# Retention and a Mish layer on one core: chunks 10 to 13 transposed by transfers, three loads moved behind them, two sums moved ahead of two scalings

## The chip, the cores and the metric

The kernel runs on one core of one Trainium2 chip. The metric is the device time of one execution in microseconds; the kernel before takes 295.73 us (median of 3 runs, 295.64 to 296.11). One more execution was taken with the hardware profiler, and all durations below come from it.

The core's engines have a queue each and run side by side: PE (TensorE, matrix products into the PSUM banks), DVE (VectorE), ACT (ScalarE), POOL (GpSimd) and SP (SyncE). Each takes its instructions strictly in the order written. POOL and SP also issue DMAs: an instruction that waits at the head of such a queue holds every DMA behind it.

## The reference

Inputs are q, k and v of shape (8, 8, 576, 64), that is batch, heads, positions, head size, and two weights of 512 x 2048 and 2048 x 512, all float32.

```python
scores = (1 / sqrt(64)) * q @ k.transpose(0, 1, 3, 2)
gamma  = 1 - 2 ** (-5 - arange(8))                 # one decay a head
Dmat   = where(i >= j, gamma ** (i - j), 0)        # causal decay
x      = (scores * Dmat) @ v                       # no softmax
x      = x.transpose(0, 2, 1, 3).reshape(4608, 512)
h      = x @ w_in
out    = (h * tanh(softplus(h))) @ w_out           # Mish between two products
```

## The kernel before

**Chunks and tiles.** Each of the 8 sequences of 576 positions is cut into four chunks of 128 and one of 64; the 64s of two sequences share a chunk. That gives 36 chunks, numbered in the order of work, and four of them make a tile of 512 tokens (nine tiles, `t`). Chunks 0 to 7 are the first chunks of all sequences and have a special path. From chunk 8 on (`N0 = 8`; the source writes chunk 10 as `N0 + 2`) the retention is done by states: a running sum of k times v for each sequence, of which every half chunk (64 positions) needs the state before it. Chunk 14 is one of the shared ones, so its loads come in half transfers (six instead of three); 12, 13, 15 and 16 are plain.

**Steps of one chunk `n`.** They are plain functions, and whoever calls them decides the order on each engine's queue, since nothing reorders the instructions.

- `load(n)` issues the DMAs of q, k and v from POOL's queue into `qkraw` and `vraw`, and remembers the last one, that of v, in `landed[n]`.
- `step_p(n)` scales q and k by their decays on DVE into `qks` (bf16; two instructions, L324).
- `step_v(n)` scales v on DVE (L331).
- `step_t(n)` turns `qks` into `qkT`, head size along the partitions. For `n < NT` (11) PE does this with eight transposes (L345) into a PSUM bank, and ACT copies them out in two parts (L346, L347). From `NT` on it is a transposing DMA from SBUF to SBUF, issued from SP (L349), which may be told to wait for another instruction (`gate`).
- `step_s(n)` makes the scores of chunks `n` and `n + 1` on PE (L363), first those of `n`, then those of `n + 1`; it needs both `qkT`.
- `step_m(n)` masks them on DVE (L369).
- `states(n)` multiplies k by v for the new states on PE (L418). It leaves a job, `sum_up`, in the list `sums`: four or so additions on DVE (L442, L452, L454) into `total`. That one leaves a cast of the totals to bf16 in the list `casts` (L457, `ssb`). `run(sums)` and `run(casts, engine)` place them in the queues.
- `outputs(n)` and `outputs_end(n)` multiply the masked scores and the states into the outputs on PE (L477, L494).
- `hold(n)` is a copy of one column of `qkT` on POOL (L512, `held`). It does nothing useful but wait for the transposing DMA of `n`, and with it POOL's queue waits.

**A visit.** `visit(n)` stands for a pair of chunks, `n` and `n + 1`, and mixes the outputs of this pair with the scores and states of the next pair on PE, in this order: first unit of `states(n + 2)`; `outputs(n)`; the first half of `outputs_end(n)`; `step_s(n + 2)`; further units; the second half of `outputs_end(n)`; the rest. The second half has to wait for all products of the first half (two halves share a bank). That wait is carried by a no-op on SP: `written` puts it there (L394), it waits for PE's products, and PE's second half waits for it. So the no-op stands in SP's queue between the transposing DMAs and the stores.

**The stretch that is changed.** After the first tile, a loop runs `u` from 0 to 23. For `u < 16` it does `g1(1, u)`, the first product and Mish (ACT, L580) of the second tile; then `g2(1, u - 16)`, a quarter of a row block of its second product. Around these the tables `ps`, `vs` and `ts_` say at which `u` which chunk gets `step_p`, `step_v` and `step_t`; the visit to 8 is at `u == 17`, that to 10 at `u == 22`. Loads of 12 and 13 are issued at `u` 4 and 8, 14 at 9, 15 at 18 and 16 at 20; a `hold(13)` stands at `u == 17`. Then the main loop runs over tiles `t` from 2 and steps `i`: the visit to 12 is at `t = 2, i = 6`, and `step_p` and `step_t` of 16 at `i = 1`. Loads of 17 and 18 wait for the Mish of products (2, 2) and (2, 3) (`gated`).

**Split products.** `halved[0]` is a count of products that `product` does in two halves of 256 columns instead of one of 512 (L548 instead of L543). The result is the same, with two instructions more (a matmul and a weight load).

Of the kernel before, what the change touches and what calls it, by code (L numbers as in the profile page):

```python
# [10 lines left out]
BF16 = mybir.dt.bfloat16  # L11
# [5 lines left out]
def kernel(  # L17
# [21 lines left out]
    P = 128  # L39
    NP = H // 2  # L40
# [3 lines left out]
    KC = d_model // P  # L44
    NCH = 4
    NPE = 18
    NT = 11
    NV = 20
    PF = 5

# [10 lines left out]
    N0 = 2 * NCH  # L61
# [11 lines left out]
    ps_sc = ctx.enter_context(tc.tile_pool(name="ps_sc", bufs=2, space=PS))  # L73
    ps_st = ctx.enter_context(tc.tile_pool(name="ps_st", bufs=1, space=PS))
# [215 lines left out]
    landed = {}  # L290

    def load(n, gate=None):
        if n >= n_chunks:
            return
        b, c = chunks[n]
        qkr = io.tile([P, 2, H, D], F32, name="qkraw")
        vr = io.tile([P, H, D], F32, name="vraw", bufs=6)
        live[n] = {"qkr": qkr, "v": vr}
        for t, src in ((qkr[:, 0], q), (qkr[:, 1], k), (vr, v)):
            if c < 4:  # L300
                ins = nc.gpsimd.dma_start(  # L301
                    out=t, in_=src[b, :, ds(P * c, P), :].rearrange("h p d -> p h d"))
                if gate is not None:
                    behind(ins, gate)
                    gate = None
            else:
                for e in range(2):
                    ins = nc.gpsimd.dma_start(
                        out=t[ds(64 * e, 64)],
                        in_=src[b + e, :, ds(512, 64), :].rearrange("h p d -> p h d"))  # L310
                    if gate is not None:
                        behind(ins, gate)
                        gate = None
        landed[n] = ins
# [21 lines left out]
    def step_t(n, gate=None):  # L336
        flat = live[n]["qks"].rearrange("p i h d -> p (i h d)")
        qk = tr.tile([P, 2, NP, P], BF16, name="qkT", bufs=6)
        if n < NT:
            if n == N0 + 2:  # L340
                tp = ps_st.tile([P, 2 * NP, P], BF16, name="st")
            else:
                tp = ps_sc.tile([P, 4 * NP, P], BF16, name="sc")[:, 0:2 * NP]
            for i in range(2 * NP):
                nc.tensor.transpose(tp[:, i, :], flat[:, ts(i, P)], ident)  # L345
            nc.scalar.copy(qk[:, 0], tp[:, 0:NP])  # L346
            later.append(lambda: nc.scalar.copy(qk[:, 1], tp[:, NP:2 * NP]))  # L347
        else:
            ins = nc.sync.dma_start_transpose(out=qk.rearrange("p i n t -> p (i n) t"), in_=flat)  # L349
            if gate is not None:  # L350
                behind(ins, gate)
        live[n]["qk"] = qk

    def step_s(n):

        sc = ps_sc.tile([P, 2, 2, NP, 64], F32, name="sc")
        for x in range(2):
            qk = live[n + x]["qk"]
            for p in range(NP):
                for e in range(2):  # L360
                    for j in range(2):
                        r, i = ds(64 * e, 64), ds(64 * j, 64)
                        nc.tensor.matmul(sc[i, e, x, p, :], lhsT=qk[r, 1, p, i], rhs=qk[r, 0, p, i],  # L363
                                         start=True, stop=True, skip_group_check=True)
        live[n]["sc"] = sc

    def step_m(n):
        sm = tr.tile([P, 2, 2, NP, 64], BF16, name="sm", bufs=2)
        nc.vector.tensor_tensor(  # L369
            sm.rearrange("p e x n i -> p (e x n) i"), live[n]["sc"].rearrange("p e x n i -> p (e x n) i"),  # L370
            mask.unsqueeze(1).to_broadcast([P, 4 * NP, 64]), op=OP.mult)
        live[n]["sm"] = sm
# [3 lines left out]
    def flush():  # L376
        while later:
            later.pop()()
# [5 lines left out]
    sums = []  # L384
    casts = []

    def behind(ins, others):

        sync = mybir.DependencyInfo(mybir.DependencyClass.Sync, mybir.DependencyReason.DATA)
        tc.add_manual_dep(ins.ins, others.ins.name, sync, reason="row halves and a bank")  # L390

    def written(products):
        sync = mybir.DependencyInfo(mybir.DependencyClass.Sync, mybir.DependencyReason.DATA)
        seen = nc.sync.nop()  # L394
        for ins in products:
            tc.add_manual_dep(seen.ins, ins.ins.name, sync, reason="row halves and a bank")
        return seen
# [64 lines left out]
    def run(jobs, *how):  # L462
        while jobs:
            jobs.pop()(*how)
# [45 lines left out]
    def hold(n):  # L510

        nc.gpsimd.tensor_copy(held[:, n % 2:n % 2 + 1], live[n]["qk"][:, 1, NP - 1, P - 1:P])  # L512

    def visit(n, banks, copies, between=None):


        units, early = states(n + 2)
        if units:
            units[0]()
        both = outputs(n, banks)  # L520
        seen = written(outputs_end(n, both, 0))
        if units:
            step_s(n + 2)
        elif between:
            between()
        for unit in units[1:early]:
            unit()
        outputs_end(n, both, 1, seen)
        for unit in units[max(early, 1):]:
            unit()  # L530
        outputs_copy(n, both, copies)
        if units:
            step_m(n + 2)

    outs = {}
    halved = [0]
# [65 lines left out]
    def stores(copy=nc.vector.tensor_copy):  # L602
        while ready:
            store(*ready.pop(), copy)
# [25 lines left out]
    def store(t, s, ops, copy):  # L630
        ot = op.tile([P, d_model], F32, name="res")
        copy(ot, ops)  # L632
        b, c = chunks[NCH * t + s]
        if c < 4:
            nc.sync.dma_start(out=out[ds(b * S + P * c, P), :], in_=ot)
        else:
            for e in range(2):
                nc.sync.dma_start(out=out[ds((b + e) * S + 512, 64), :], in_=ot[ds(64 * e, 64), :])

    def att(n, steps):  # L640
        if n >= n_chunks:
            return
        for step in steps:
            {"P": step_p, "V": step_v, "T": step_t}[step](n)
# [69 lines left out]
    for i in range(nF):  # L714
        for step in steps.get(i, "").split():
            n = int(step[1])
# [14 lines left out]
    queued = [4 * NCH]  # L731
# [5 lines left out]
                queued[0] += 1  # L737


    ps = {0: (0,), 4: (1,), 8: (2,), 11: (5,), 14: (6,), 23: (7,)}  # L740
    vs = {0: (0,), 5: (1,), 18: (4,), 19: (5,)}
    ts_ = {3: (0,), 7: (1,), 10: (3, 4), 12: (2,), 17: (5,), 18: (6,)}
    for u in range(24):
        j, w = divmod(u, 4)
        halved[0] = 2 if 0 < u < 9 or 11 < u < 16 else 4 if 15 < u < 18 else 0
        if u == 9:
            att(N0 + 2, "V")
            att(N0 + 3, "PV")
            att(N0 + 4, "P")
            load(N0 + 6)  # L750
        for n in ps.get(u, ()):
            att(N0 + n, "P")
        if u == 11:
            step_m(N0)
        for n in vs.get(u, ()):
            att(N0 + n, "V")
        if u == 18:
            load(N0 + 7)
        if w == 0 and j in (1, 2, 5):
            if j < 5:  # L760
                load(N0 + j + 3)
            else:
                load(N0 + j + 3)
                queued[0] += 1
        if u == 10:
            units, early = states(N0)
            seen = written(units[0]())
            step_s(N0)
            units[1]()
            units[2](seen)  # L770
            run(sums)
        elif u == 17:
            visit(N0, ((ps_o, "ops"), (ps_h, "hp")), (act, act))
            run(sums)
        elif u == 22:
            visit(N0 + 2, ((ps_h, "hp"), (ps_h, "hp")), (act, dve))
        elif u == 23:
            att(N0 + 7, "T")
        if u == 20:
            stores(act)  # L780
        if u in (13, 20):
            run(casts, dve if u == 13 else act)
        for n in ts_.get(u, ()):
            step_t(N0 + n, landed[N0 + 6] if n == 3 else None)
        if u == 17:
            hold(N0 + 5)
        stores()
        if u < nF:
            g1(1, u, 2 if u == 0 else 1)
            flush()  # L790
        else:
            g2(1, u - nF)
# [3 lines left out]
    for t in range(2, nT + 1):  # L796
        for i in range(nF):
            n, w = NCH * (t + 1) + i // 8 * 2, i % 8
# [19 lines left out]
            if w == 7 and n + 4 <= NPE + 2:  # L818
                step_t(n + 5, newest[0])
# [74 lines left out]
```

## Time and profile before

| | |
|---|---|
| median of 3 runs | 295.73 us (295.64 to 296.11) |
| the profiled execution, its own time | 296.05 us |
| its span, first to last instruction | 294.3 us |
| PE busy | 288.2 us (98%) |
| DVE, ACT, POOL busy | 140.7, 125.0, 125.0 us (48%, 42%, 42%) |
| granted TensorE clock | 1.0 |
| DMA, mean over the span | 164 GB/s, 48.23 MB |
| loop over `u` in the trace | about 47 to 73.5 us |
| visits to 8, 10 and 12 on PE | from 64.5, 70.5 and 82.5 us |

Lines of the profile read like this: start or busy time in microseconds, the engine, the line of the source, the operation, the tiles as out<-in, and the count; in brackets the idle time of the engine ahead of the instruction and what ended it. `SPq` is SP's queue; the duration of a DMA there or on POOL is that of its issue, not of the transfer. "DMA to landing" is the time from the issue to the last byte's arrival.

### The profile page before, as it was taken

How to read it: one execution, taken by the hardware profiler on the slowest of the kernel's cores; microseconds unless marked ns; L12 is line 12 of the kernel's file. 1: busy time of each engine (PE TensorE's matmuls, PEld its weight loads, DVE VectorE, ACT ScalarE, POOL GpSimd, SP SyncE). 2: the span in 40 equal slices, each digit the busy share in tenths (PEclk: the TensorE clock that was granted, in tenths of full speed). 3: DMA queues.
4: the chain of work that ended last, by engine and by line, in shares of the span. 5: the costliest groups of instructions: out<-in, count | busy, mean ns of one | idle time of the engine just before them, and what ended most of it. 6: DMA issues, size and time to landing. Idle time of an engine off the chain costs nothing.

```text
span 294.3 us, 7942 instructions
## 1 busy us (share of the span) xinstructions
PE 288.2 (98%) x3485; PEld 160.5 (55%) x3485; DVE 140.7 (48%) x252; ACT 125.0 (42%) x206; POOL 125.0 (42%) x164
## 2 busy tenths in 40 slices
PE   8999999999899999999999999999999999999995
PEld 5666887665557454547545454545454544444443
DVE  6851659787763838454645454535453321000011
ACT  4866126764545534443444434343435333333200
POOL 8944769705267294955484536392020000000000
PEclk9999999999999999999999999999999999999999
DMA  7999999958798999899576838374222111011121
GB/s 157 236 202 205 205 327 357 328 136 178 220 249 236 148 243 225 248 158 309 131 209 176 247 90 256 94 222 120 70 64 71 38 38 65 9 36 44 62 74 71
DMA packets 47235, 48.23 MB, mean 164 GB/s; under 512 B 29152, under 2 KB 36320, under 8 KB 47200
## 3 DMA queue, kind: packets, MB, share of 16 engines
q0 software_dynamic: 15120, 31.20, 41.7%
q1 hardware_dynamic: 31936, 16.32, 22.6%
q8 instruction: 27, 0.44, 0.7%
q10 hardware_dynamic: 144, 0.20, 0.2%
q14 instruction: 8, 0.07, 0.1%
HBM read 37.75 MB, written 9.44 MB: 160 GB/s over the span
## 4 chain that ended last, share of the span: by engine, by line
PE 90%; DVE 4%; DMA 3%; ACT 1%; POOL 1%; issue 0%; POOLq 0%; DVEq 0%
PE hp L543 38%; PE ops L543 30%; PE hp L548 7%; PE ops L548 3%; DMA qkraw<-in_k_dram 2%; PE sc L363 1%; PE hp L624 1%; PE hp L494 1%; PE st L548 1%; PE sc L418 1%; PE hp L477 1%; DMA qkT<-qks 1%; DVE total L454 1%; PE st L418 1%; PE sc L200 1%; PE sc L222 1%
## 5 line engine op out<-in xcount | busy, mean ns | idle before, releaser
L543 PE MATMUL hp<-xT,w_in_t 128*128 128x512 bf16 (+1 forms) x508 | 126.0, 376 | 0.9 <-ACT gT L580 0.9
L580 ACT ACTIVATE gT<-hp 128x512 bf16<-128x512 f32 x142 | 84.6, 597 | 95.1 <-PE hp L543 94.2
L543 PE MATMUL ops<-w_out_t,gT 128*128 128x512 bf16 x416 | 102.5, 379 | 0.0
L543 PEld LDWEIGHTS <-w_in_t 128*128 128x128 bf16 x511 | 49.9, 98 | 50.9 <-issue 0.2
L543 PEld LDWEIGHTS <-gT 128*128 128x128 bf16 x463 | 44.3, 98 | 50.8
L632 DVE COPY res<-ops 128x512 f32<-128x512 f32 x28 | 19.3, 689 | 85.3 <-PE ops L543 85.3
L324 DVE TENSOR_TENSOR qks<-qkraw,gqk 128x512 bf16<-128x512 f32 x56 | 36.9, 710 | 3.7 <-DMA qkraw<-in_k_dram 3.7
L331 POOL TENSOR_TENSOR vs<-vraw,gv 128x512 bf16<-128x512 f32 x16 | 16.8, 1070 | 24.0 <-PE hp L477 23.9
L301 POOL DMA_DIRECT2D qkraw<-in_q_dram x24 | 21.5, 894 | 12.2 <-ACT gT L580 5.4
L506 DVE CAST xT<-hp 128x512 bf16<-128x512 f32 x13 | 9.0, 691 | 31.1 <-PE hp L494 31.1
L301 POOL DMA_DIRECT2D qkraw<-in_k_dram x24 | 21.4, 894 | 0.6 <-DMA vpair<-in_v_dram 0.6
L301 POOL DMA_DIRECT2D vraw<-in_v_dram x24 | 21.2, 883 | 1.1 <-DMA w_out_t<-in_moe_w_out_dram 0.8
L548 PEld LDWEIGHTS <-gT 128*128 128x128 bf16 x194 | 18.6, 98 | 4.1
L548 PE MATMUL hp<-xT,w_in_t 128*128 128x256 bf16 x136 | 20.7, 272 | 0.0
L506 ACT CAST xT<-hp 128x512 bf16<-128x512 f32 x14 | 8.2, 587 | 28.9 <-PE hp L494 28.9
L548 PEld LDWEIGHTS <-w_in_t 128*128 128x128 bf16 x138 | 13.5, 98 | 9.8 <-issue 1.8
L512 POOL COPY held<-qkT 128x1 bf16<-128x1 bf16 x9 | 1.9, 212 | 39.1 <-DMA qkT<-qks 39.1
L369 DVE TENSOR_TENSOR sm<-sc,mask 128x1024 bf16<-128x1024 f32 x14 | 17.0, 1214 | 1.4 <-PE sc L363 1.4
L454 DVE TENSOR_TENSOR total<-sc,total 128x256 f32<-128x256 f32 x40 | 16.9, 422 | 1.0
L457 ACT CAST ssb<-total 128x768 bf16<-128x768 f32 (+3 forms) x13 | 11.6, 893 | 5.3 <-DVE total L454 5.3
L548 PE MATMUL ops<-w_out_t,gT 128*128 128x256 bf16 x96 | 12.4, 273 | 0.0
L543 PE MATMUL hp<-w_out_t,gT 128*128 128x512 bf16 x45 | 11.0, 379 | 0.0
(132 smaller groups left out, 240.1 us busy)
## 6 DMA issues: line engine op xcount, KB each, us to landing
out_dram<-res SPq DMA_DIRECT2D x31, 256.0 KB, 2.9
qkraw<-in_q_dram POOLq DMA_DIRECT2D x24, 256.0 KB, 4.7
qkraw<-in_k_dram POOLq DMA_DIRECT2D x24, 256.0 KB, 4.9
vraw<-in_v_dram POOLq DMA_DIRECT2D x24, 256.0 KB, 5.0
w_out_t<-in_moe_w_out_dram POOLq DMA_DIRECT2D x4, 512.0 KB, 12.2
gT<-in_k_dram POOLq DMA_DIRECT2D x8, 128.0 KB, 6.5
gT<-in_v_dram POOLq DMA_DIRECT2D x2, 512.0 KB, 6.0
w_in_t<-in_moe_w_in_dram POOLq DMA_DIRECT2D x2, 512.0 KB, 10.1
```

Source lines behind the costliest of these rows:

```text
L301: ins = nc.gpsimd.dma_start(out=t, in_=src[b, :, ds(P * c, P), :].rearrange("h p d -> p h d"))
L324: nc.vector.tensor_tensor(slots[:, :, y], heads[:, :, y], factors[:, :, y].unsqueeze(3).to_broadcast([P, NP, 2, D]), op=OP.mult)
L331: engine.tensor_tensor(vs, live[n]["v"], gv[:, c, :].unsqueeze(2).to_broadcast([P, H, D]), op=OP.mult)
L369: nc.vector.tensor_tensor(sm.rearrange("p e x n i -> p (e x n) i"), live[n]["sc"].rearrange("p e x n i -> p (e x n) i"), mask.unsqueeze(1) ...
L418: ins = nc.tensor.matmul(to, lhsT=ks, rhs=vs, start=(x is not None or j == 0 and p == 0), stop=True, skip_group_check=True)
L454: nc.vector.tensor_tensor(new[:, k], st[:, j, x], total[b], op=OP.add)
L457: casts.append(lambda copy: copy(lows[:, 0:k], new[:, 0:k]))
L506: copy(xts[t][:, :, ds(P * s, 2 * P)].rearrange("p h (x j i) -> p j h x i", x=2, j=2)[:, j], both[j])
L543: newest[0] = nc.tensor.matmul(to, lhsT=w, rhs=x, start=first, stop=last)
L548: nc.tensor.matmul(to[:, ts(j, n)], lhsT=w, rhs=x[:, ts(j, n)], start=False, stop=False, skip_group_check=True)
L580: done = nc.scalar.activation(gts[t][:, f, :], hp, AX.Mish)
L632: copy(ot, ops)
```

## The change

- `NT` goes from 11 to 10: chunk 10 is transposed by a DMA like those after it. The branch that gave it a bank of its own goes with it.
- The transposing DMAs of 10, 11 and 12 are called at `u == 10`, that of 13 at `u == 12`. That of 10 waits for the landing of v of 13 (`landed[N0 + 5]`). Before, that of 11 waited for v of 14, and that of 13 was called at `u == 17` behind the visit to 8.
- `hold(13)` moves from `u == 17` to `u == 12`. Behind it, at `u == 12`, come the loads of 14, 15 and 16.
- `step_p` of 14 moves from `u == 14` to 23, and stands there with that of 15. Ahead of both, the sums of the visit to 10 are run.
- The transposing DMAs of 14 and 15 are both called at `u == 23`; that of 14 waits for v of 16.
- `halved` is set otherwise: six more products are split.

```diff
-    NT = 11
+    NT = 10
...
         if n < NT:
-            if n == N0 + 2:
-                tp = ps_st.tile([P, 2 * NP, P], BF16, name="st")
-            else:
-                tp = ps_sc.tile([P, 4 * NP, P], BF16, name="sc")[:, 0:2 * NP]
+            tp = ps_sc.tile([P, 4 * NP, P], BF16, name="sc")[:, 0:2 * NP]
...
-    ps = {0: (0,), 4: (1,), 8: (2,), 11: (5,), 14: (6,), 23: (7,)}
+    ps = {0: (0,), 4: (1,), 8: (2,), 11: (5,), 23: (6, 7)}
     vs = {0: (0,), 5: (1,), 18: (4,), 19: (5,)}
-    ts_ = {3: (0,), 7: (1,), 10: (3, 4), 12: (2,), 17: (5,), 18: (6,)}
+    ts_ = {3: (0,), 7: (1,), 10: (2, 3, 4), 12: (5,), 23: (6, 7)}
     for u in range(24):
         j, w = divmod(u, 4)
-        halved[0] = 2 if 0 < u < 9 or 11 < u < 16 else 4 if 15 < u < 18 else 0
+        halved[0] = 2 if 0 < u < 9 else 4 if 11 < u < 18 else 2 if 17 < u < 21 else 0
         if u == 9:
             att(N0 + 2, "V")
             att(N0 + 3, "PV")
             att(N0 + 4, "P")
-            load(N0 + 6)
+        if u == 23:
+            run(sums)
         for n in ps.get(u, ()):
             att(N0 + n, "P")
...
-        if u == 18:
-            load(N0 + 7)
-        if w == 0 and j in (1, 2, 5):
-            if j < 5:
-                load(N0 + j + 3)
-            else:
-                load(N0 + j + 3)
-                queued[0] += 1
+        if w == 0 and j in (1, 2):
+            load(N0 + j + 3)
...
-        elif u == 23:
-            att(N0 + 7, "T")
...
         for n in ts_.get(u, ()):
-            step_t(N0 + n, landed[N0 + 6] if n == 3 else None)
-        if u == 17:
+            step_t(N0 + n, landed[N0 + {2: 5, 6: 8}[n]] if n in (2, 6) else None)
+        if u == 12:
             hold(N0 + 5)
+            for n in (6, 7, 8):
+                load(N0 + n)
+            queued[0] += 1
         stores()
```

## The prediction

> **What bounds the kernel now.** I read the page first (PE busy 98% of the span, so only PE's gaps and PE's own work can pay), then the chain of waits in order of time, 56 to 86 us, which is the stretch that the diff touches:
>
> ```profile
> 65.44 0.35 PE sc L363 x16
> ...
> 69.73 0.89 POOL qkraw L301
> 70.62 5.12 DMA qkraw<-in_k_dram
> ...
> 78.41 0.83 ACT ssb L457
> 79.24 0.51 ACT gT L580
> ```
>
> PE leaves the chain twice. At 65.44 it takes up chunk 11's transposed tile, a transfer issued at 62.58, as that lands. From 69.73 the chain runs over the load of 15, its scaling on VectorE, and the totals and cast queued behind that, to ScalarE, which is then late with a bank of `hp`. The timeline of PE prices the second wait; it also shows chunk 10's eight transposes (L345) and the visit to chunk 12 (from 82.49):
>
> ```profile
> 59.50 0.61 PE L345 MATMUL st<-ident,qks 128*128 128x128 bf16 x8
> 59.95 0.38 PE L543 MATMUL hp<-xT,w_in_t 128*128 128x512 bf16 x1
> ...
> 79.79 0.38 PE L543 MATMUL hp<-xT,w_in_t 128*128 128x512 bf16 x1 [0.95 <-ACT gT L580]
> ...
> 83.02 0.45 PE L363 MATMUL sc<-qkT 64*64 64x64 bf16 x32
> ```
>
> The timelines of POOL and SP give the queues (columns: start, duration, what, wait before it):
>
> ```profile
> 52.48 0.88 POOL L301 DMA_DIRECT2D vraw<-in_v_dram  x1 [0.33 <-DMA qkraw<-in_q_dram]
> ...
> 69.20 0.40 POOL L512 COPY held<-qkT 128x1 bf16<-128x1 bf16 x1 [10.14 <-DMA qkT<-qks]
> ...
> 74.12 0.88 POOL L301 DMA_DIRECT2D vraw<-in_v_dram  x1
> ...
> 101.05 1.37 POOL L308 DMA_DIRECT2D qkraw<-in_q_dram  x2 [6.45 <-PE ops L543]
> ```
>
> ```profile
> 62.58 6.53 SPq L349 DMA_TRANSPOSE qkT<-qks  x4
> ```
>
> And the landing of single transfers: the v of 13 (issued 52.48), the v of 16 (74.12), and the transposing transfer of 16 (issued 80.11), which runs beside the loads of 17:
>
> ```profile
> DMA to landing us min/median/max: 8.1/8.1/8.1
> ```
>
> ```profile
> DMA to landing us min/median/max: 4.8/4.8/4.8
> ```
>
> ```profile
> DMA to landing us min/median/max: 4.3/4.3/4.3
> ```
>
> Below, T10 is chunk 10's transposing transfer, and so on.
>
> **Removed from PE.** The eight transposes of 10: 59.50 to 59.95, -0.45 us. Their two copies (0.59 and 0.58) leave ScalarE, which waits for PE there, so nothing. Six more products are split in two; eight halves take 0.87 in the chain against 0.86 for four whole products: +0.02.
>
> **Totals ahead of scaling.** The totals of 12 (L454 and L452, 1.34 + 0.42) no longer stand behind the wait for k of 15. They start after the mask product that ends at 73.8 and end near 75.6; the cast falls behind ScalarE's second gT of that stretch (75.41 to 76.0). The stall of 0.95 goes: -0.95. What is late next is the visit to 12, below.
>
> **Four transfers ahead of SP's no-op.** T10 waits for v of 13: 52.48 + 8.1 = 60.6. SP takes 1.24 to 1.38 for each issue (the first two here 62.58, 63.96; the third took 2.27). All four tiles are scaled by 61.4, so the issues stand at 60.6, 62.0, 63.35 and 64.7, the last ending at 66.0. T11 lands at 64.8, when PE wants it (64.7): nothing there. But the visit to 8 has a no-op on SP (L394) between its two halves of `outputs_end`, and PE's second half waits for it. Before, T13 was issued behind that no-op; now it is ahead. So the second half starts at 66.06 where it started at 65.72: **+0.34 net**, in which the 0.45 is already used up. Bounds: -0.2 (v of 13 lands 0.5 sooner with no load of 14 behind it) and +1.3 (one issue takes 2.27). I take the usual issue. PE then comes to the visit to 12 at 82.49 + 0.34 + 0.02 - 0.95 = 81.9.
>
> **Loads of 14 to 16 behind T13.** POOL's queue is in order: the copy `held` waits for T13, and nine transfers' worth of loads stand behind it. T13 lands 2.8 after its issue (as the first of the four did), at 67.5; copy and first issue put q of 14 at 68.1. Chunk 14 is six half transfers at 0.68 (chunk 21's same shape: 101.05 to 105.11, 4.06), so q of 15 is issued at 72.2. From q of 15's issue to v of 16's landing took 74.12 + 4.8 - 69.73 = 9.2: **v of 16 lands at 81.3**, where it landed at 78.9. Bounds: six issues (4.4) and the shortest landing of a load in the trace, 2.8: 79.4; or the pace from 101.05 on, where the same nine loads took 14.9: 83.0. I take the middle row, since it is the same two chunks at the same place.
>
> By the Trainium skill, DMA: Bandwidth & Descriptors, section Anatomy of one DMA, a transfer costs about 2.0 us plus its bytes at 436 GB/s, an estimate of 2.6 for these 256 KB. The rows here are 4.8 and 8.1 in a full queue; by the skill's figure v of 16 would land near 79.2 and the sum would be about that of the second rival.
>
> **T14 and T15 behind v of 16.** This is where it is paid. T14 is issued at 81.4, T15 at 82.75 (one issue, 1.35). POOL is free at 77.4 and the gT that gates 17 is done near 77.7, so loads of 17 and 18 run beside both, as beside T16 now: 4.3 to landing, **T15 at 87.05**. Bounds: 2.75 (T15 now, from 77.20 with hardly anything beside it) and 6.0 (the longest, issued 111.77). PE takes up T15 in the second half of `step_s(14)`, in order, with nothing else to do: now 83.02 + 0.13 = 83.15, then 87.1. Behind T15 on SP stand a store, T16 and this visit's no-op, free at 86.2, so no further cost; on VectorE the scaling of 16 waits for k of 16 and holds vs of 15 to about 83.0, a wait inside the same one.
>
> **Sum.** PE after this visit is back to back to the end, so its place there is the total: 87.1 - 83.15 = +3.95 (the -0.95, -0.45 and +0.34 all lie inside it). On the profiled execution, 296.05 (span 294.3 plus 1.75 around it): 300.0. The median is 0.32 below that execution: **299.6 us**. With both ends at once: T15 at 79.4 + 0.1 + 1.35 + 2.75 = 83.6 gives 296.2; at 83.0 + 0.1 + 1.35 + 6.0 = 90.45 it gives 303.
>
> **Rivals.**
> 1. *Faster: the transfers are in time.* If T15 lands by 82.0, only 0.34 + 0.02 - 0.95 = -0.6 is left: 295.1; without the no-op's cost 294.3. It decides from v of 16 landing at 77.9 or sooner. For it: the loads of 14 no longer hold those of 13, and everything could start earlier. Against: nine issues alone, 4.06 + 4.39 from 68.1, put v of 16's issue at 76.55, and no load landed under 2.8. Chance 0.05.
> 2. *About the same: transfers land as if alone.* Loads at 2.8 and T15 at 2.75 give 83.6: 296.2. Against it: six of six loads from 101.05 to 109.49 of full size took over 4. Chance 0.08.
> 3. *Slower still: PE's clock falls.* In the windows the granted clock is 1.0 everywhere, but no idle time of PE there exceeds 1 us; here some 5 us between 81.9 and 87 hold only 0.7 us of small products. The trace's clock record starts full at 4.9 although PE starts at 1.26, and falls to 0.5 only after PE's end: 3.7 us at half speed would cost 1.8, so 301.4. Chance 0.10. The Trainium skill, TensorE: Matmul & The Clock Gate, section HAM oscillation, states that PE idle for more than about 3.4 us falls back to half its clock; no gap of the trace tests this.
> 4. *The transposing transfers disturb each other.* An instruction fetch (queue q8) lay beside the third of the four; its issue took 2.27 and a landing 4.4. If that meets T12 or T13 again, the no-op is 1.0 later and the loads 1 to 1.6: 300.9. Chance 0.12.
> 5. *No effect:* excluded but for 0.01; the order of the changed program has four transfers and `held` where I put them.
>
> The remaining 0.64 is the forecast.
>
> **How the numbers follow.** 0.2% is 0.6 us, about what a measurement of this kernel can tell. Slower by more: 0.64 + 0.10 + 0.12, and a quarter of rival 2: 0.88. Within: the rest of rival 2 and rival 5: 0.07. Faster: 0.05. The range leaves out rival 1 and the outer ends: 296.3 (the lower bounds together) to 302.0 (the forecast with one transfer at its upper bound, or rival 3 with a late landing).
>
> **What would show it.** Right: POOL's `held` near 67.6; loads of 16 landing at 80 to 82; SP's transfers of 14 and 15 issued only then; in the visit to 12 a wait of PE of 3 to 5 us in all ahead of and within L360 (old L363), ended by SP's transfers; no wait for ACT gT near 79; a wait of about 0.8 in the visit to 8, ended by SP. Wrong: T15 landing before 83, or a visit to 12 without a gap; or a new gap of PE elsewhere that I have not named.

## The result and the profile after

The changed kernel takes 308.55 us (median of 6, 304.39 to 311.0) against 295.69 us: 1.0393 of before, 95% interval 1.033 to 1.0455. The forecast was 299.6, at most 302.0. The profiled execution is the shortest of the six, 304.39 us with a span of 302.7. Executions of this kernel differ by several us where those of before differ by 0.8; the ratio is over those that lie close to the fastest, and where a trace below is of a longer one, its time is given.

The place of the loss is the one forecast. PE's timeline through the visit to 12, which before has no wait in it:

```profile
83.57 0.22 PE L415 MATMUL sc<-vs,qks 64*64 64x64 bf16 x2 [2.71 <-DVE vs L331]
...
88.33 0.43 PE L360 MATMUL sc<-qkT 64*64 64x64 bf16 x16 [4.07 <-DMA qkT<-qks]
88.99 0.43 PE L360 MATMUL sc<-qkT 64*64 64x64 bf16 x16 [0.24 <-DMA qkT<-qks]
...
91.46 3.81 PE L540 MATMUL hp<-xT,w_in_t 128*128 128x512 bf16 x10
```

Three waits in brackets: vs of 15, then the tile of 14 (4.07), then that of 15 (0.24 more). The last row holds ten products in 3.81 us that take 2.3 at full clock. The queues that lead there, POOL's and SP's:

```profile
52.01 0.88 POOL L301 DMA_DIRECT2D vraw<-in_v_dram  x1 [0.44 <-DMA qkraw<-in_q_dram]
67.97 0.19 POOL L509 COPY held<-qkT 128x1 bf16<-128x1 bf16 x1 [15.07 <-DMA qkT<-qks]
68.50 1.45 POOL L308 DMA_DIRECT2D qkraw<-in_q_dram  x2 [0.34 <-DVE total L451]
...
77.03 0.88 POOL L301 DMA_DIRECT2D vraw<-in_v_dram  x1
```

```profile
59.25 5.39 SPq L346 DMA_TRANSPOSE qkT<-qks  x4
68.79 0.34 SPq L632 DMA_DIRECT2D out_dram<-res  x1
81.82 4.40 SPq L346 DMA_TRANSPOSE qkT<-qks  x2
```

And how long the transfers of 14 (issued 81.8) and of 15 (issued 83.2) took to land, followed by the stretches around the visit (the columns after the length are the busy times of PE, PEld, DVE, ACT, POOL, then granted clock, DMA share, GB/s):

```profile
DMA to landing us min/median/max: 6.5/6.5/6.5
```

```profile
DMA to landing us min/median/max: 5.7/5.7/5.7
```

```profile
80.40:84.20 3.80, 1.09 (x67) 0.72 (x65) 2.50 (x4) 0.07 (x1) 2.77 (x4) 1.00 0.96 279
84.20:94.50 10.30, 5.66 (x82) 2.72 (x77) 4.55 (x8) 1.18 (x2) 0.00 (x0) 0.50 0.72 178
94.50:300.00 205.50, 202.72 (x2293) 103.47 (x2317) 82.12 (x134) 78.60 (x128) 71.19 (x88) 1.00 0.49 132
```

The clock is at half for 10.2 us, from 84.2 to 94.5. The difference in span is 302.7 - 294.3 = 8.4. PE takes up 15's tile at 88.99 instead of 83.15, +5.84. It comes to a product behind the half clock at 96.40 instead of 88.03, +8.37, so 2.5 us were lost between the two points, where the products are spaced 0.427 instead of 0.216 until the clock is back. Nothing behind that differs. That product before and after:

```profile
88.03 1.03 PE L543 MATMUL ops<-w_out_t,gT 128*128 128x512 bf16 x4
```

```profile
96.40 1.03 PE L540 MATMUL ops<-w_out_t,gT 128*128 128x512 bf16 x4
```

### The profile page after: what moved, and what is told of

It reads as the page before. It is cut to its first block, busy times and chain, and to the rows that moved or that the text cites. A ratio compares the mean times of both kernels' runs of the same rounds, so it can differ in the third digit from the quotient of the medians.

```text
span 302.7 us, 7898 instructions
## 1 busy us (share of the span) xinstructions
PE 287.0 (95%) x3444; PEld 161.7 (53%) x3483; DVE 140.5 (46%) x252; ACT 124.4 (41%) x204; POOL 124.7 (41%) x164
## 4 chain that ended last, share of the span: by engine, by line
PE 89%; DMA 4%; DVE 3%; issue 2%; POOL 2%; ACT 0%
PE hp L540 37%; PE ops L540 29%; PE hp L545 7%; PE ops L545 3%; DMA qkraw<-in_k_dram 2%; DMA qkT<-qks 2%; PE sc L360 1%; PE ops L170 1%; PE hp L621 1%; PE hp L491 1%; PE sc L415 1%; PE st L545 1%; PE hp L474 1%; POOL qkraw L308 1%; DVE sm L226 1%
## 5 line engine op out<-in xcount | busy, mean ns | idle before, releaser
L540 PE MATMUL hp<-xT,w_in_t 128*128 128x512 bf16 (+1 forms) x489 | 124.5, 379 | 0.8
L540 PE MATMUL ops<-w_out_t,gT 128*128 128x512 bf16 x401 | 100.1, 381 | 2.1 <-issue 2.1
L540 PEld LDWEIGHTS <-gT 128*128 128x128 bf16 x457 | 43.8, 98 | 50.0 <-issue 0.5
L545 PEld LDWEIGHTS <-gT 128*128 128x128 bf16 x206 | 19.8, 98 | 4.6
L545 PE MATMUL ops<-w_out_t,gT 128*128 128x256 bf16 x100 | 13.1, 273 | 0.2
L415 PE MATMUL sc<-vs,qks 64*64 64x64 bf16 x384 | 9.9, 198 | 2.7 <-DVE vs L331 2.7
## 6 DMA issues: line engine op xcount, KB each, us to landing
w_in_t<-in_moe_w_in_dram POOLq DMA_DIRECT2D x2, 512.0 KB, 10.8
```

What stands on the lines that cost most here:

```text
L415: ins = nc.tensor.matmul(to, lhsT=ks, rhs=vs, start=(x is not None or j == 0 and p == 0), stop=True, skip_group_check=True)
L540: newest[0] = nc.tensor.matmul(to, lhsT=w, rhs=x, start=first, stop=last)
L545: nc.tensor.matmul(to[:, ts(j, n)], lhsT=w, rhs=x[:, ts(j, n)], start=False, stop=False, skip_group_check=True)
```

## The experiments

Theories after the result: (a) the two late transfers are the loss, because they run among the loads of 17 and 18; (b) the clock's fall behind the wait adds to it; rivals: the gate or the loads' place alone, a wait elsewhere in the longer executions, a cost of the clock that is only apparent. T10 to T17 are the transposing transfers of chunks 10 to 17, as in the prediction.

**The changed kernel once more.** No edit.

> The changed kernel once more, for a second trace of it. Theory: the visit to 12 waits for vs of 15 (about 2.7 us) and longer for the transposed tiles of 14 and 15, more than the 4.1 us of the first trace if this execution is longer than 304.4 us; behind it the granted clock is 0.5 for three or four stretches of 3.4 us. Rival (a wait elsewhere makes the executions of 306 to 311): a gap of PE of over 1 us outside the visit to 12.

306.73 and 309.5 us; the trace is of the first.

```profile
82.17 0.22 PE L415 MATMUL sc<-vs,qks 64*64 64x64 bf16 x2 [1.03 <-DVE vs L331]
86.38 0.43 PE L360 MATMUL sc<-qkT 64*64 64x64 bf16 x16 [3.51 <-DMA qkT<-qks]
92.57 0.43 PE L360 MATMUL sc<-qkT 64*64 64x64 bf16 x16 [5.76 <-DMA qkT<-qks]
```

The loads were earlier here (T14 issued at 80.4, T15 at 81.8), and vs of 15 with them, yet T14 took 5.9 us to land and T15 10.8. Behind the first 12 us no other wait is over 0.4 us. So these two executions differ by how long T15 takes, not by a further wait; the half clock lasted 10.2 us again. DMA over T15's flight, 81.7 to 92.6, in 40 slices:

```profile
GB/s 180 150 241 183 264 283 208 92 46 200 453 301 421 241 257 308 266 233 132 103 93 108 102 145 57 43 163 95 78 188 139 159 277 46 41 317 322 282 185 21
```

From the 19th slice on (86.6 us) the sum of both kinds is mostly below 160 GB/s until 91, where loads alone ran at 279 in the row of the first trace.

**A second hold: loads of 17 and 18 behind T15.**

```diff
+        if u == 23:
+            hold(N0 + 7)
         stores()
```

> The changed kernel with one edit: a second hold on POOL, behind the transfer of 15, so that the loads of 17 and 18 start only when that has landed. Theory (a transposing transfer and ordinary loads that are in the DMA engines together slow each other): 14's transfer still starts when v of 16 lands (80 to 82) and 15's 1.4 later, but 15 now lands 2.8 after its issue, at 84.5 to 86.5, where it took 5.7 in the changed kernel and 13.2 with idle products; the wait for the tiles falls from 4.1 us to 1 to 2.5, the clock stays 1.0, 299 to 301 us, and the executions agree within 1 us or so. Rival (the transfers are slow by themselves when two follow each other, or the wait is the loads' lateness alone): 15 lands 4 us or more after its issue and the time stays at 304 us or more.

302.15 us (300.23 to 303.4; trace of 303.4), 1.0196 (1.0157 to 1.0235). T14 and T15 are issued at 82.4 and 83.8, later than in either trace above, and T15 lands after:

```profile
DMA to landing us min/median/max: 2.7/2.7/2.7
```

```profile
84.15 0.26 PE L415 MATMUL sc<-vs,qks 64*64 64x64 bf16 x2 [2.86 <-DVE vs L331]
86.56 0.43 PE L360 MATMUL sc<-qkT 64*64 64x64 bf16 x16 [0.93 <-DMA qkT<-qks]
...
102.30 0.32 PE L360 MATMUL sc<-qkT 64*64 64x64 bf16 x16 [1.51 <-DMA qkT<-qks]
```

One edit, nothing else moved ahead of T15: its 5.7 and 10.8 became 2.7, T14's 6.5 and 5.9 became 2.7 too, and 6 us of the loss and half of the spread are gone. That shows (a). The rival that two transfers slow each other falls, since the two still follow each other by 1.4 us. The size was off, since the loads held back now meet T17, which took 7.7 (the wait at 102.30), and the clock fell all the same, for 6.8 us from 83.4, within the wait for vs:

```profile
83.40:90.20 6.80, 4.60 (x131) 2.92 (x132) 3.04 (x5) 0.59 (x1) 2.83 (x5) 0.50 0.76 188
```

**The changed kernel without the gate of T14.**

```diff
-            step_t(N0 + n, landed[N0 + {2: 5, 6: 8}[n]] if n in (2, 6) else None)
+            step_t(N0 + n, landed[N0 + 5] if n == 2 else None)
```

> The changed kernel with one edit: the transfer of 14 doesn't wait for the landing of v of 16. Theory: the transfer of 14 is issued near 76 and that of 15 as soon as 15 is scaled (k of 15 lands near 79, so near 80.3), landing at 84.5 to 86; the wait for vs of 15 (2.7 us) stays, the wait for the tiles shrinks from 4 us to 1 to 2: 299 to 301 us, and the clock falls for a shorter time or not at all. Rival (the loads beside them slow the transfers, the gate does not matter): the tile of 15 lands at 88 or later and the time stays at 304 us or more.

299.36 us (298.26 to 303.01), 1.0096 (1.0068 to 1.0124). T15 was issued at 78.1, 5 us sooner, and took 7.3 to land, so it came at 85.4 instead of 89.0:

```profile
82.95 0.22 PE L415 MATMUL sc<-vs,qks 64*64 64x64 bf16 x2 [1.43 <-DVE vs L331]
85.45 0.32 PE L360 MATMUL sc<-qkT 64*64 64x64 bf16 x16 [1.68 <-DMA qkT<-qks]
```

The time and the landing are as expected, and the clock stayed 1.0 in the trace. The way there is not: T15 went out 2 us sooner than I expected, and it flew longer, since the loads of 17 start at 78.3 and it ran among them all the same. So 9 of the 13 us go with the gate because the transfers are issued sooner, not because they land faster; they meet loads with and without it.

**The loads of 14 to 16 and the hold back in their old places, no gate.**

```diff
         if u == 9:
...
+            load(N0 + 6)
-        if w == 0 and j in (1, 2):
+        if u == 18:
+            load(N0 + 7)
+        if w == 0 and j in (1, 2, 5):
-        if u == 12:
+        if u == 17:
             hold(N0 + 5)
-            for n in (6, 7, 8):
-                load(N0 + n)
```

> The change with the loads of 14, 15 and 16 and the hold back at their old places (14 at u = 9, hold at 17, 15 at 18, 16 at 20) and without the wait of 14's transfer for v of 16; all else as changed. Theory: the loads' place is the whole loss; the visit to 12 shows no wait, the clock stays 1.0, and what is left is the totals' 0.95 less a wait of 0 to 2 us in the visit to 8, since the transfers of 10 to 13 now run beside 14's loads: 294.5 to 296.5 us. Rival (transposing 10 to 13 by transfers ahead of the visit to 8 costs by itself): 297 us or more, with a gap in the visit to 8 of over 2 us.

300.15 us (298.07 to 304.07; trace of 298.07), 1.0111 (1.0081 to 1.0142): my expectation fell. In the visit to 8 there is a wait of only 0.43, so T10 to T13 ahead of it cost next to nothing and the rival falls too. But in the visit to 12:

```profile
85.27 0.32 PE L360 MATMUL sc<-qkT 64*64 64x64 bf16 x16 [3.04 <-DMA qkT<-qks]
```

T15 was issued at 79.0 and took 6.3. The loads of 17 now start at 78.4 instead of 80.4: the Mish that gates them is no longer late, since the stall near 79 is gone. This suggests that the wait that the change removes had kept these loads off T15 and T16; the next run starts them early without removing it.

**Before, with the loads of 17 and 18 earlier.**

```diff
-    gated = {(2, 2): 17, (2, 3): 18}
+    gated = {(2, 0): 17, (2, 1): 18}
```

> The kernel before with one edit: the loads of 17 and 18 wait for the Mish of products (2, 0) and (2, 1) instead of (2, 2) and (2, 3), so they follow those of 16 at once, near 75.3 instead of 80.4. Theory (transfers and loads together slow each other): the transfer of 15 (issued 77.2, landed 2.75 later before) and that of 16 (4.3) now run among loads and take 5 us or more; PE waits in the visit to 12 for 15's tile, 297 to 305 us, and executions differ by several us. Rival (earlier loads only help): nothing waits, 295.5 to 296 us.

298.15 us (295.8 to 302.48, 10 executions), 1.0042 (1.0016 to 1.0068). The trace is of an execution of 301.33: T15, issued at 77.4, took 9.4 us, and PE waited 3.2 us for it:

```profile
86.86 0.38 PE L363 MATMUL sc<-qkT 64*64 64x64 bf16 x16 [3.17 <-DMA qkT<-qks]
```

As expected: the same collision, made in the kernel before by one edit to a gate.

**The change with idle products against the clock's fall, without and with the second hold.**

```diff
     def states(n):
...
         st = ps_sc.tile([P, 2, 2, NP, 64], F32, name="sc")
+        if n == 14:
+            for _ in range(11):
+                nc.tensor.matmul(st[:, 0], lhsT=zeros[:, 0:P], rhs=zeros, start=True, stop=True)
```

(The first kernel has 15 more ahead of the scores of 14.)

> The changed kernel with idle products (zeros, 128x512) on PE in the visit to 12: 11 ahead of its first unit and 15 ahead of the scores, in banks that are overwritten afterwards, about 2.4 and 3.2 us of work in waits of 2.7 and 4 us. Theory (the clock falls because PE idles): the clock stays 1.0, the waits stay, and the time is that of the waits alone, 5.9 us over before: 301.5 to 302.5 us, with less spread from execution to execution. Rival (the clock's fall costs nothing, or zeros do not count as work): 304 us or more.

309.31 us (305.35 to 310.03; trace of 310.03). This tells nothing of the clock's price: T15 took 13.2 us in the trace, PE waited 7.4 behind the idle products, and the clock fell there.

> The changed kernel with the hold behind the transfer of 15 and with 11 idle products (zeros, 128x512, about 2.4 us) on PE ahead of the first unit of the visit to 12, where it waits 2.9 us for vs of 15; they write a bank that is overwritten. Theory (the clock falls because PE idles, and what that costs is the products behind the visit at half speed, five of them in the trace of the hold alone): the clock stays 1.0, the waits stay as they are, about 1 us less than with the hold alone: 300 to 301.5 us. Rival (the clock falls all the same, or it costs nothing): 301.5 to 303 us.

303.52 us (301.12 to 305.24; trace of 303.51), no better than the hold alone. In the visit to 12 the clock stayed 1.0, as the theory has it:

```profile
80.00:88.00 8.00, 7.41 (x159) 4.32 (x160) 4.30 (x7) 1.78 (x3) 2.84 (x5) 1.00 0.65 158
```

But T17 then took 8.3 us among loads, PE waited 1.71 for ACT and 2.15 for T17, and the clock fell behind that, at 102. With the hold alone the clock fell at this place, with products in the same wait it did not (mean granted clock 0.994 in all four executions, 0.988 to 0.989 in the four with the hold alone), so here PE's idling lowered it; but no time was won by preventing that once. Its price stays the one read from the first trace after, 2.5 us.

**Before, with the totals ahead alone.**

```diff
+        if u == 23:
+            run(sums)
```

> The kernel before with one edit, the totals of 12 run ahead of the scaling of 15 at u = 23. Theory: PE's wait of 0.95 us for ACT near 79 goes and nothing takes its place: 294.7 us (294.5 to 295.0). Rival (a wait takes its place, for instance for vs of 15 or the tile of 15 in the visit to 12, since PE comes there 0.95 sooner): 295.3 to 295.8.

296.67 us (295.03 to 308.29; trace of 295.93), 0.9997 (0.9974 to 1.002). The rival's mechanism holds, though the median lies above its range: the wait for ACT is gone, and another has half its length (timeline of PE), while POOL shows a likely reason why the executions now spread, up to 308.29 us:

```profile
82.35 0.22 PE L418 MATMUL sc<-vs,qks 64*64 64x64 bf16 x2 [0.50 <-DVE vs L331]
```

```profile
78.64 0.88 POOL L301 DMA_DIRECT2D qkraw<-in_q_dram  x1 [3.20 <-ACT gT L580]
```

17's loads start 1.8 us sooner than before; in this trace T15 took 4.5 to land and T16 6.4, where they took 2.7 and 4.3.

**Three attempts at a faster kernel.** All scale v of 14 and 15 ahead of q and k of 16. The first two are before with the totals ahead, one with a hold behind T15, one with the loads of 17 and 18 gated by products (2, 4) and (2, 5); the third is the kernel with the loads back, gated by (2, 5) and (2, 6).

```diff
-            if w in ((3, 4) if n + 2 < NPE else (0, 1)):
+            if n == 12:
+                if w == 1:
+                    att(n + 2, "V")
+                    att(n + 3, "V")
+                    att(n + 4, "PT")
+            elif w in ((3, 4) if n + 2 < NPE else (0, 1)):
...
-    gated = {(2, 2): 17, (2, 3): 18}
+    gated = {(2, 4): 17, (2, 5): 18}
```

> The kernel before with three edits: the totals of 12 ahead of the scaling of 15 (u = 23), the scaling of v of 14 and 15 ahead of that of 16, and a hold on POOL behind the transfer of 15, so that the loads of 17 wait for it. Theory: the wait of 0.95 us near 79 goes, the wait of 0.5 us for vs of 15 that took its place in the kernel with the totals alone goes as well, and 15's transfer lands 2.8 us after its issue in every execution: 294.6 to 295.2 us. Rival (the loads of 17 come too late or the transfer of 16 meets them): a wait in the visit to 14, 296 us or more.

> The kernel before with three edits: the totals of 12 ahead of the scaling of 15 (u = 23), the scaling of v of 14 and 15 ahead of that of 16, and the loads of 17 and 18 behind the Mish of products (2, 4) and (2, 5) instead of (2, 2) and (2, 3), so that they start near 80.5 as before although PE is 0.95 us ahead. Theory (the stall of 0.95 us kept the loads of 17 off the transfers of 15 and 16; with the loads held back by other means the gain can be kept): no wait near 79 or in the visit to 12, 294.6 to 295.3 us, and executions within 1 us or so. Rival (the transfers meet the loads anyway, or 17 comes late to the visit to 14): 296 us or more.

> The change with the loads of 14 to 16 and the first hold at their old places and without the wait of 14's transfer for v of 16, as in the run with the loads back, and in addition the scaling of v of 14 and 15 ahead of that of 16 and the loads of 17 and 18 behind the Mish of products (2, 5) and (2, 6). Theory (the wait of 3 us in the visit to 12 that was left with the loads back came from the loads of 17 among the transfers of 15 and 16): 15 lands 2.8 to 4 us after its issue, no wait in the visit to 12, 294.5 to 295.8 us. Rival (the transfers of 14 and 15 at u = 23 are too late by themselves): a wait of 1 us or more in the visit to 12, 296.5 us or more.

Measured: 296.65 us, 1.0019 (0.9996 to 1.0042); 296.13 us, 1.0003 (0.9974 to 1.0032); 297.61 us, 1.0028 (1.0002 to 1.0054). In the traces the collision is gone from the visit to 12 in all three (T15 lands in 3.7, 3.5 and 3.3 us, no wait there), and the second has a span of 293.7, 0.6 below before. But in the first and third T17 meets the loads that were put off, and PE waits 0.6 and 0.8 for it in the visit to 14; and the executions of all three spread over 3 to 6 us. All three medians lie 0.8 to 1.8 us above the range expected, and no version beat the kernel before. A part of such a spread is not the edits': the kernel before, executed 22 times beside the last two, ran from 295.44 to 298.48 us, and once 302.21.

## Why the prediction was wrong, by its own steps

- *Removed from PE, and the totals ahead:* right. In the trace after there is no wait for ACT near 79, and the transposes are gone. PE comes to the visit to 12 at 80.6, where 81.9 was forecast, mostly since the wait of the next item did not come.
- *Four transfers ahead of SP's no-op:* right in kind, wrong in size and of no weight. v of 13 landed at 59.2 instead of 60.6: it was issued 0.5 sooner and flew 0.9 shorter, with no loads of 14 behind it (with them back it landed at 60.1). So T10 was issued at 59.25 and the four issues ended at 64.64, just before PE wanted the no-op. The second half of `outputs_end` starts at 64.75 instead of 66.06. The bound of 0.5 us on v of 13 was too narrow.
- *Loads of 14 to 16 behind T13:* right. First load 68.50 (68.1), v of 16 landed 81.7 (81.3), T14 issued 81.82 (81.4), T15 83.22 (82.75). T13 itself took 4.4 in this trace, where an instruction fetch lay beside it (65.8 to 66.7, queue q8). That is what rival 4 feared; the earlier start made up for it. In the repeat T13 took 2.75.
- *T14 and T15 in flight among loads:* **this term failed.** I took 4.3 us for T15, T16's row, with 6.0 as the most, and gave T14 no flight that could bind. Measured for T15: 5.7, 10.8 and, with idle products, 13.2; and 2.7 with the loads held back. T14 took 6.5, more than my upper bound, and ended the longest wait of the profiled execution. In the trace of before T16's data moved at 81.1 to 82.4 us and the loads beside it began to move theirs only at 82.2: its row was a near miss and not the price of a collision. The repeat, 2.3 us longer than the profiled execution, is longer by this term; of the executions near the median, 308.55, there is no trace. Their mean granted clock, 0.977 to 0.982 against 0.983, allows for at most 1.9 us of their 4 (an estimate, 0.006 of 308 us), so half of it or more must be waiting.
- *The clock (rival 3, chance 0.10):* put at nothing in the sum, **it came**, in every trace of the change that kept T14's gate. Rival 3 had counted one stretch of 3.7 us at half speed, 1.8 us; it was 10.2, of which PE worked through about half, 2.5. Nor did the fall need a single wait of more than 3.4 us: with the second hold it came within one of 2.9. By the Trainium skill, TensorE: Matmul & The Clock Gate, Part 1, the clock gate watches PE in a free-running window of 3413 ns; the lengths here, 10.24, 6.83 and 3.41, are whole multiples of that, so the trace agrees.
- *The price of a load:* the Trainium skill (DMA: Bandwidth & Descriptors, Anatomy of one DMA) gives 2.0 us plus bytes at 436 GB/s for a load issued from POOL, an estimate of 2.6 for 256 KB. The trace does not agree for a full queue: v of 16 took 4.7, and no load of q, k or v of that size landed under 3.4 in the trace of before. The 2.8 us in my lower bound, the row of a half transfer, was too short as well. The sum went by the row of 4.8, which held.

So the sum had the right path and two wrong sizes. On the profiled execution it gave 300.0 and 304.39 was measured: PE took up T15 at 88.99 instead of 87.1, 1.9 us, and the half clock cost 2.5. What makes T15 take 5.7 in one execution and 10.8 in the next was not settled; the traces differ in how the packets of the two kinds meet.

## What to carry to other kernels

A row for a transfer "beside" others is a price only if the two were truly in the engines together: look at when the data moved, not at the issues, and if no row shows a real overlap, say that the upper end is open. Before a wait is removed, ask what it holds back: here a late ScalarE, which cost PE 0.95 us, also delayed the gate of two chunks' loads and so kept them off two transposing transfers. A wait of 2 us or more on PE should be priced with a possible fall of the clock: in these traces it came with waits from 2.1 us on, though not with one of 3.0.

## What the runs showed of the hardware

- A transposing transfer of 256 KB landed 2.7 us after its issue alone, and 5.5 to 13.2 us after it when ordinary loads were in flight for all of that time. The loads slow as well: in the flight of 10.8 us both kinds together moved mostly less than 160 GB/s for over 4 us, against 279 for loads just before a transfer's data began to move.
- With no load beside it T13 took 2.7 to 2.8 us in four traces of the changed order, and 4.3 to 4.8 in four others, in which an instruction fetch (queue q8, 0.9 to 1.8 us) began during its flight. That the fetch is the cause was not shown: in one of the quick ones it began 0.3 us before the landing and delayed nothing.
- The granted clock fell within or just behind PE's waits of 2.9, 3.2, 3.5 and 7.4 us, 0.6 us behind one of 2.7 and 1.3 us behind one of 2.1; but not at one of 3.0 us in another kernel, nor at 1.4 and 1.7 us with 0.8 us between. It stayed at half for 3.4 to 10.2 us. Idle products on zeros, 2.5 us of them, kept it at 1.0 through the visit to 12.
- Loads queued behind a load delay that one's last byte: v of 13 landed 7.0 to 7.3 us after its issue in the six traces without 14's loads behind it and 7.7 to 9.2 in the seven with them.
